# Seven copies out of PSUM moved from ScalarE to VectorE in the last four slots of an attention and soft-MoE kernel

## The chip, the cores and the metric

The kernel runs on one core of one Trainium2 chip. The metric is the device time of one execution, in microseconds (us). A core has TensorE (PE, matrix products into PSUM), VectorE (DVE), ScalarE (ACT), GpSimd (POOL) and SyncE (SP), each of which works through its own instructions in order; semaphores order them against each other. In this program POOL also issues every load, through one queue of DMA transfers (`gdma`).

## What is computed

Attention whose softmax has one more term in its denominator, then a soft mixture of experts with 8 experts of 4 slots each (32 slots):

```python
scores = scale * q @ k.T                       # 8 batches, 12 heads, 448 rows, 64 wide
m = max(scores, -1);  e = exp(scores - m)
x = (e / (sum(e, -1) + exp(-m) + 1e-9)) @ v    # then [3584, 768], heads side by side
logits = x @ phi                               # [3584, 32]
d = softmax of logits over all 3584 rows;  c = softmax of logits over the 32 slots
slot_input = d.T @ x
slot_out[expert] = relu(slot_input[expert] @ w1[expert]) @ w2[expert]
out = c @ slot_out
```

The softmax over all rows is made batch by batch with a running maximum; the weighted sum `d.T @ x` is corrected by a factor each time the maximum moves.

## The kernel before

**Pairs and slots.** The 96 heads are taken as 48 pairs n (`NPAIR`), six to a batch (`PB`), three to a group (`NP`, so `NG` is 16). The main loop (L556) has a slot s for every pair, and each slot has a first half (y=0) and a second half (y=1). For its pair a slot makes the scores with the maxima subtracted in PSUM (`Bk`: L300, then L303) and takes their exp on ACT (L306, four exps in the first half, three in the second). `AV` (L331) multiplies them with v into the one buffer of the pool psV. The maxima come from an earlier pass over the scores (`A`, with `reduce_max` on DVE at L229 and L238), which runs ahead of the slots and so has ended before the last four.

**What follows a pair.** `N1(n)` (L343) copies the pair's results out of psV; `N2(n)` divides them (the reciprocals L352 and L353 on DVE, the products L359, L367 and L368 on POOL, but on DVE for n from 44 on, see `on_pool` at L335). In slot s, N1(s-1) stands in the first half; N2(s-1) stands right behind it when it is on DVE, and at the end of the second half when it is on POOL. `PX(s-2)` in the second half turns the divided x over with four matmuls (L391) into a PSUM buffer of the pool psB, and L397 copies that to the tile `xT`. `W2` and `W3` turn a group's maxima into rows: L265 and L266 on PE, the copy at L271, two small exps at L274 and L277; group 16, the last, has its turn in slot 44.

**Buffers.** psB has four buffers handed out in turn. In the last slots the requests of one slot are: two for `Bk(s,0)`, two for `Bk(s,1)`, two for `Bk(s,2)`, one for `Bk(s,3)`, then one for `PX(s-2)` (in slot 44 `W2` takes one before it). So the buffer of `PX` is asked for again by the fourth request behind it, which is the second head's matmul of `Bk(s+1,1)`. psV has a single buffer: `AV` of the next pair waits for N1.

**Work hung between.** `post` (L511) holds the steps of the logits and of the running softmax of the batch that has just ended. For batch 6 they fall into slots 44 to 47: the logits and `c_max` (first half of 44), `l_turn` and `c_sub` (second half of 44), `s_max` and `d_sub` (first half of 45), the exps and `corr` (first half of 46), `s_mm` and `s_add` (second half of 46), `c_turn` (second half of 47, four short DVE instructions L475 to L479). In a half they are written ahead of PX. Batch 7, the last, follows in `last`: `l_mm` needs the columns of xT of pairs 42 to 47.

**Weights into freed space.** The weights of w2 for experts 3 to 7 are loaded into the tile R, which holds the attention's buffers until then. `part_at` (L554) and L629, L630, L644, L645 say which part goes when; each transfer waits until what lay there has been read. The parts are counted here in units of 192 KB (one index z of `load_part`). Those that matter below: five units after slots 44 and 45; five units after slot 46, into space that ends with x0, which `s_mm` of batch 6 reads (L469); two after slot 47; eight (L629, L630) after the last `AV` (they cover e2, e1 and vp1); four (L644) after the last read of xT; three (L645) after the last read of x1 by the last `s_mm`. The last matmuls of the experts (`slots(1)`, L669) read the end of that last part.

**The end.** `hidden`, `turn` and `slots` run the experts, and L728 to L739 make and store the output.

The pieces that the change touches are short:

```python
t = psm.tile([128, S], BF16, tag="mT", name="mT")
nc.scalar.copy(t, st["ps_m"][:, 0:S])                                    # W3, L271
(nc.scalar.copy if on_pool(n) else nc.vector.tensor_copy)(u, src)        # N1, L343
nc.scalar.copy(xT[:, pb, :], pss[0])                                     # PX, L397
```

Of the kernel before, what the change touches and what calls it, by code (L numbers as in the profile page):

```python
# [31 lines left out]
def kernel(  # L32
# [10 lines left out]
    nc = tc.nc  # L43
    B, H, S, D = q.shape
# [9 lines left out]
    NPAIR = B * PB  # L54
    NG = NPAIR // NP
# [40 lines left out]
    xT = part("xT", 0, KC * 512).rearrange("p (j s) -> p j s", j=KC)  # L96
# [25 lines left out]
    with ExitStack() as at:  # L122
# [62 lines left out]
        st = {"e2": 0}  # L185
# [82 lines left out]

        def W3(g):
            t = psm.tile([128, S], BF16, tag="mT", name="mT")  # L270
            nc.scalar.copy(t, st["ps_m"][:, 0:S])  # L271
            mT[g] = t
            e = psm.tile([128, NP, 7], F32, tag="ec", name="ec", bufs=3)
            nc.scalar.activation(e[:, :, 0:6].rearrange("p l (i h) -> p i l h", i=3),  # L274
                                 ngm[g][:, 0:18].rearrange("p (i l h) -> p i l h", i=3, h=2),
                                 AF.Exp, scale=scale)
            nc.scalar.activation(e[:, :, 6], ngm[g][:, 18:21], AF.Exp, scale=scale)  # L277
            ec[g] = e
# [56 lines left out]
        on_pool = lambda n: n < NPAIR - 4  # L335

        def N1(n):
            src = av[n][:, 0:7 * W65].rearrange("p (s c) -> p s c", c=W65)
            if n == NPAIR - 1:
                us[n] = src  # L340
                return
            u = ubuf[:, n % 2, :].rearrange("p (s c) -> p s c", c=W65)
            (nc.scalar.copy if on_pool(n) else nc.vector.tensor_copy)(u, src)  # L343
            us[n] = u

        def N2(n):
# [28 lines left out]
        def keep_busy(n):  # L375

            if "idle" not in st:
                st["idle"] = pb_("ps_idle")
            for _ in range(n):
                nc.tensor.matmul(st["idle"], ident, w_sb["w1", 0][:, 0, 0:512], start=True, stop=True)  # L380

        def PX(n):
            b, pb = divmod(n, PB)
            x, c = xb[b % 2], slice(pb * 128, pb * 128 + 128)
            two = n == NPAIR - 1
            pss = [pb_("ps_x") for _ in range(1 + two)]
            for i in range(4):
                if i == 3 and two:
                    keep_busy(1)
                o = (i % 2 if two else i) * 128  # L390
                nc.tensor.matmul(pss[i // 2 if two else 0][:, o:o + 128], x[:, i, c], ident if i < 3 else ident2,  # L391
                                 start=True, stop=True)
            if two:
                nc.scalar.copy(xT[:, pb, 0:256], pss[0][:, 0:256])
                nc.vector.tensor_copy(xT[:, pb, 256:512], pss[1][:, 0:256])
            else:
                nc.scalar.copy(xT[:, pb, :], pss[0])  # L397

# [142 lines left out]
        T(2)  # L543
        W2(0)
        W3(0)
        As(1)
        for nm in "qk":
# [8 lines left out]
        for s in range(NPAIR + 1):  # L556
            for y in range(2):
# [15 lines left out]
                if y == 0:  # L573
                    if 0 <= s - 1:
                        for i in (2, 3):
                            AV(s - 1, i, range(3))
                else:
                    if 2 <= s < NPAIR - 6:
                        T(s + 6)
                    g = (s + 1) // 3  # L580
                    if (s + 1) % 3 == 0 and g < NG:
                        W2(g + 1)
                        W3(g + 1)
                    if s < NPAIR:
                        for i in (0, 1):
                            AV(s, i, range(3))
                if 2 * s + y in post:
                    post[2 * s + y]()
                if y and 0 <= s - 2 < NPAIR - 2:
                    PX(s - 2)  # L590
                if y == 0:
                    if 0 <= s - 1:
                        for i in range(4):
                            AV(s - 1, i, [3])
                        N1(s - 1)
                        if not on_pool(s - 1):
                            N2(s - 1)
                else:
                    if 0 <= s - 1 and on_pool(s - 1):
                        N2(s - 1)  # L600
                As(early)
                if hs == 1:
                    W2(1)
                    W3(1)
                if hs == 4:
                    W1(2)
            g = (s + 10) // 3
            if s == 1 or s % 3 == 2:
                g = 3 if s == 1 else g
# [3 lines left out]
            g = (s + 9) // 3  # L613
# [16 lines left out]
        load_part(15, 0, 1)  # L630
        nc.vector.reduce_max(fold, ident.rearrange("p (i s) -> p s i", i=4), axis=AX.X)
        PX(NPAIR - 2)
        keep_busy(2)
        last[1]()
        PX(NPAIR - 1)
        keep_busy(1)
        last[2]()
# [50 lines left out]
        pss = [pb_("ps_so") for _ in range(2)]  # L688
# [26 lines left out]
    with ExitStack() as ex:  # L715
        psO = ex.enter_context(tc.tile_pool(name="psO", bufs=4, space=PSUM))
        for bp in range(B // 2):
# [4 lines left out]
            for t0 in range(0, 7, 2):  # L722
                ts = range(t0, min(t0 + 2, 7))
                pss = [psO.tile([128, 2, 512], F32, tag="o", name="ps_o") for _ in ts]
# [45 lines left out]
```

## Time and profile before

| what | value |
|---|---|
| time, median of 3 runs (lowest to highest) | 324.32 us (324.28 to 325.05) |
| the profiled execution | 326.12 us, span 324.3 us |
| busy: PE, DVE, ACT, POOL | 281.0, 257.5, 250.3, 199.3 us |
| in 250 to 270 us: PE, DVE, ACT, POOL | 18.0, 9.9, 17.8, 10.4 us |
| in the same 20 us: DMA | 143 GB/s, the mean of four windows of 5 us (122, 156, 173, 120) |
| in 270 to 285 us: DMA | 204 to 211 GB/s |
| slots 44, 45, 46, 47 begin (first L300) | 250.3, 255.7, 259.8, 265.05 us |
| output phase begins (first L728) | 294.31 us |

A span runs from the first to the last instruction of the profiled execution; the execution's own time has 1.8 us around it. Start times of the trace are given in us from the span's start. In a row of the time line the first number is the start, the second the duration of the merged group, and in brackets stands the idle time before it with what ended it. A chain of waits is read from its end: each piece was released by the one above it.

### The profile page before, as it was taken

Reading aid. Unit: us, or ns where it says so; the run is one execution under the profiler, and the core shown is the slowest. Engines: PE = TensorE matmul, PEld = TensorE weight load, DVE = VectorE, ACT = ScalarE, POOL = GpSimd, SP = SyncE. Lnnn points to the kernel's source line nnn. Section 1 sums busy time; section 2 is a strip of 40 time slices with the busy share of each in tenths; the row PEclk is TensorE's granted clock in tenths of the full one; section 3 lists DMA queues with packets and bytes.
Section 4 is the critical chain, followed back from the end, with each engine's and each line's share of the span. In section 5 each row is a group of like instructions: output and inputs, shape, how many; then the busy total and the mean of one; then the engine's idle time right before and its main releaser. Section 6 shows DMA issues by size and latency. Waiting matters only on the chain.

```text
span 324.3 us, 12137 instructions
## 1 busy us (share of the span) xinstructions
PE 281.0 (87%) x5052; PEld 162.5 (50%) x5054; DVE 257.5 (79%) x601; ACT 250.3 (77%) x547; POOL 199.3 (61%) x399
## 2 busy tenths in 40 slices
PE   3898899999999999999999999999899887977800
PEld 1444456556656565556656565656565444441100
DVE  4779999998999899899999998999899355327910
ACT  2456699998999899989998999899989984317800
POOL 8641778888787869666978688777747825000000
PEclk9999999999999999999999999999999999998555
DMA  6990599999999999866999999999646889973997
GB/s 86 140 133 3 86 205 152 202 166 193 173 174 176 176 187 150 135 98 113 149 196 132 196 158 193 148 200 146 111 51 99 140 137 194 210 131 160 434 424 340
DMA packets 42438, 54.30 MB, mean 167 GB/s; under 512 B 2576, under 2 KB 35344, under 8 KB 42000
## 3 DMA queue, kind: packets, MB, share of 16 engines
q0 software_dynamic: 41376, 42.52, 84.7%
q1 hardware_dynamic: 1008, 11.01, 8.1%
q8 instruction: 39, 0.64, 0.7%
q14 instruction: 15, 0.12, 0.1%
HBM read 85.03 MB, written 11.01 MB: 296 GB/s over the span
## 4 chain that ended last, share of the span: by engine, by line
PE 35%; DVE 29%; ACT 18%; issue 6%; DMA 4%; POOL 3%; POOLq 0%; ACTq 0%
DVE mx L229 18%; ACT R L306 9%; PE ps_av L331 8%; PE ps_a L225 6%; PE ps_b L300 6%; PE ps_t L203 5%; DMA R<-in_moe_w_dram 4%; PE ps_b L303 4%; ACT R L206 3%; DVE mx L238 3%; ACT R L397 2%; PE ps_o L728 2%; DVE R L208 2%; ACT W L734 2%; PE ps_s L469 2%
## 5 line engine op out<-in xcount | busy, mean ns | idle before, releaser
L229 DVE TENSOR_REDUCE mx<-ps_a 128x1 f32<-128x448 f32 x288 | 160.9, 614 | 13.2 <-PE ps_a L225 12.7
L306 ACT ACTIVATE R<-ps_b 128x448 bf16<-128x448 f32 x336 | 158.6, 563 | 12.9 <-PE ps_b L303 8.6
L300 PE MATMUL ps_b<-R 64*128 64x448 bf16 (+1 forms) x384 | 83.2, 360 | 3.2 <-ACT R L397 3.0
L303 PE MATMUL ps_b<-mT,sel 64*128 64x448 bf16 (+1 forms) x384 | 79.0, 354 | 0.0
L225 PE MATMUL ps_a<-R 64*128 64x448 bf16 x288 | 68.6, 369 | 5.8 <-DVE mx L229 3.4
L331 PE MATMUL ps_av<-R 128*128 128x65 bf16 (+1 forms) x1536 | 64.9, 196 | 2.0 <-DVE ubuf L343 1.3
L359 POOL TENSOR_TENSOR R<-ubuf,rec 128x384 bf16<-128x384 f32 x44 | 36.1, 821 | 49.2 <-DVE rec L353 39.6
L331 PEld LDWEIGHTS <-R 128*128 128x128 bf16 (+1 forms) x1536 | 50.7, 101 | 27.5 <-issue 23.4
L203 PEld LDWEIGHTS <-R 64*64 64x64 bf16 x1344 | 31.4, 113 | 19.6 <-issue 9.6
L203 PE MATMUL ps_t<-ident,R 64*64 64x64 bf16 x1344 | 31.9, 198 | 7.7 <-DMA R<-in_q_dram 4.0
L397 ACT CAST R<-ps_x 128x512 bf16<-128x512 f32 x47 | 28.3, 601 | 10.3 <-PE ps_x L391 10.3
L303 PEld LDWEIGHTS <-sel 64*128 64x128 bf16 (+1 forms) x384 | 21.5, 98 | 24.5 <-issue 17.8
L300 PEld LDWEIGHTS <-R 64*128 64x128 bf16 (+1 forms) x384 | 19.7, 97 | 27.4 <-issue 22.9
L238 DVE TENSOR_REDUCE mx<-ps_a 128x1 f32<-128x448 f32 x48 | 29.5, 614 | 0.6 <-PE ps_a L235 0.3
L206 ACT COPY R<-ps_t 128x896 bf16<-128x896 bf16 x20 | 18.4, 919 | 11.0 <-PE ps_t L203 11.0
L343 ACT COPY ubuf<-ps_av 128x455 f32<-128x455 f32 x44 | 25.2, 572 | 2.1 <-PE ps_av L331 1.0
L225 PEld LDWEIGHTS <-R 64*128 64x128 bf16 x288 | 17.8, 94 | 15.0 <-issue 4.1
L368 POOL TENSOR_TENSOR R<-ubuf,rec 128x128 bf16<-128x128 f32 x44 | 17.5, 398 | 3.7
L235 PE MATMUL ps_a<-R 64*64 64x448 bf16 x96 | 18.7, 386 | 0.6 <-DVE mx L229 0.6
L391 PE MATMUL ps_x<-ident,R 128*128 128x128 bf16 x192 | 18.7, 219 | 0.0
L245 POOL TENSOR_SCALAR R<-mx 64x6 bf16<-64x6 f32 (+5 forms) x51 | 13.5, 264 | 8.4 <-DVE mx L229 4.8
L108 POOL DMA_DIRECT2D R<-in_moe_w_dram x15 | 10.7, 717 | 12.3 <-PE ps_s L469 7.2
(121 smaller groups left out, 364.8 us busy)
## 6 DMA issues: line engine op xcount, KB each, us to landing
W<-in_moe_w_dram POOLq DMA_DIRECT2D x22, 768.0 KB, 9.4
out_dram<-W SPq DMA_DIRECT2D x3, 2688.0 KB, 11.2
R<-in_v_dram POOLq DMA_DIRECT2D x32, 192.0 KB, 4.5
R<-in_q_dram POOLq DMA_DIRECT2D x15, 336.0 KB, 6.9
R<-in_k_dram POOLq DMA_DIRECT2D x15, 336.0 KB, 7.8
R<-in_moe_w_dram POOLq DMA_DIRECT2D x3, 768.0 KB, 9.4
out_dram<-W SPq DMA_DIRECT2D x3, 768.0 KB, 4.3
R<-in_moe_w_dram POOLq DMA_DIRECT2D x1, 1344.0 KB, 13.3
```

Of the source, the lines that this page charges most:

```text
L203: nc.tensor.transpose(ps[r, a, c:c + 64], src[r, pl, tok * D:(tok + 1) * D], ident[r, r])
L206: nc.scalar.copy(t, ps)
L225: nc.tensor.matmul(pss[hl][:, 0:S], t[r, 0, i * 128:(i + 1) * 128], t[r, 1, :], start=True, stop=True)
L229: nc.vector.reduce_max(mx[g][:, c:c + 1], pss[hl][:, 0:S], axis=AX.X)
L238: nc.vector.reduce_max(mx[g][:, c:c + 1], ps[:, 0:S], axis=AX.X)
L300: nc.tensor.matmul(outs[hl], t[rs[hl], 1, cols], t[rs[hl], 0, :], start=True, stop=False)
L303: nc.tensor.matmul(outs[hl], sel[rs[hl], 2 * pl + hl:2 * pl + hl + 1].to_broadcast([64, m]), mT[mg(n)][rs[hl], :], start=False, stop=True)
L306: nc.scalar.activation(e, p[:, 0:S], AF.Exp, scale=scale)
L331: nc.tensor.matmul(o, eT[n, i, hl][:, qc], vp[g % 2][:, 2 * pl + hl, i, 0:W65], start=(i == 0 and u == 0 and hl == 0), stop=(i == 3), skip ...
L343: (nc.scalar.copy if on_pool(n) else nc.vector.tensor_copy)(u, src)
L359: eng.tensor_mul(x[:, 0:3, c:c + 128].rearrange("p i (h d) -> p i h d", h=2), u[:, 0:6, 0:D].rearrange("p (i h) d -> p i h d", h=2), rec[: ...
L397: nc.scalar.copy(xT[:, pb, :], pss[0])
```

## The change

Three copies get a condition of their own. The copy of a group's maxima's rows goes to DVE for the last group (g = 16: one instruction). The copy of a pair's results goes to DVE from n = 43 on, where it was from n = 44 on (one more instruction; pairs 44 to 46 were there already, and pair 47 has no copy). The copy of transposed x goes to DVE for n = 42 to 46 (five instructions); pair 47 keeps its two half copies, one on each engine. Where the products of N2 run is not changed.

```diff
         def W3(g):
             t = psm.tile([128, S], BF16, tag="mT", name="mT")
-            nc.scalar.copy(t, st["ps_m"][:, 0:S])
+            (nc.scalar.copy if g < NG else nc.vector.tensor_copy)(t, st["ps_m"][:, 0:S])
...
-            (nc.scalar.copy if on_pool(n) else nc.vector.tensor_copy)(u, src)
+            (nc.scalar.copy if n < NPAIR - 5 else nc.vector.tensor_copy)(u, src)
...
-                nc.scalar.copy(xT[:, pb, :], pss[0])
+                (nc.scalar.copy if n < NPAIR - 6 else nc.vector.tensor_copy)(xT[:, pb, :], pss[0])
```

## The prediction

> **What bounds the kernel now.** I read the busy shares of the page first, then the stretch that the change touches (250 to 272 us) in windows, then the chain of waits there, then the time lines of DVE, ACT and PE, and last the DMA rate. The windows (PE, PEld, DVE, ACT, POOL, granted clock, DMA share, GB/s):
>
> ```profile
> 250.00:255.00 5.00, 4.42 (x78) 2.42 (x75) 1.08 (x4) 4.97 (x12) 4.33 (x12) 1.00 0.77 122
> 255.00:260.00 5.00, 4.60 (x75) 2.56 (x73) 3.07 (x11) 4.64 (x13) 3.88 (x8) 1.00 0.96 156
> 260.00:265.00 5.00, 4.09 (x80) 2.42 (x76) 2.70 (x10) 3.95 (x10) 0.23 (x1) 1.00 1.05 173
> 265.00:270.00 5.00, 4.88 (x92) 2.94 (x89) 3.07 (x12) 4.24 (x9) 1.98 (x3) 1.00 0.79 120
> ```
>
> ACT looks full and DVE half idle, so a move seems free. But the chain says who waits for whom:
>
> ```profile
> 256.24 0.19 PE ps_b L300
> 256.43 0.35 PE ps_b L300
> ...
> 259.64 0.24 PE ps_x L391 x4
> ...
> 259.90 0.58 ACT R L397
> 260.48 1.76 ACT R L306 x4
> ...
> 262.99 0.64 DVE ubuf L343
> ...
> 263.67 0.52 PE ps_av L331 x12
> 264.19 0.69 PE ps_s L469 x28
> ...
> 277.54 13.89 DMA R<-in_moe_w_dram
> ```
>
> Two things are to be seen. First, a slot here is a latency chain through PE, ACT and DVE, about 4.1 to 5.4 us long. The exps of a slot begin at most 0.1 us after their matmuls: in slot 45 L303 ends at 256.24 and the exp starts at 256.27, in slot 46 260.34 and 260.38, in slot 47 265.60 and 265.63. So ACT has hardly a queue in front of them that the change could empty. In slot 44 W2 waits for POOL (its last maxima row ends at 254.77, L266 starts at 254.82), which no moved copy feeds. Second, the second head's L300 of Bk(s+1,1) waits for the buffer that PX used: it starts at 256.43, 260.53 and 265.79, 0.05 us behind the ends of the L397 copies (256.38, 260.48, 265.73). PE is in order, so everything behind it waits too. In groups the page has the same:
>
> ```profile
> L300 PE MATMUL ps_b<-R 64*128 64x448 bf16 (+1 forms) x384 | 83.2, 360 | 3.2 <-ACT R L397 3.0
> ```
>
> The end is then set by the load of the last weights, 13.89 us in the chain. Those DMAs run without a gap at about 207 GB/s, or 0.95 us a unit, from 267.5 to 288.4 us (22 units), so their end follows their first gate, s_mm in slot 46 (issue at 265.06, data from about 267.5: 2.45 us later). PE, which works through the experts meanwhile, is close behind:
>
> ```profile
> 288.75 1.97 PE L669 MATMUL ps_so<-R,W 128*32 128x384 bf16 x43
> 291.47 1.14 PE L669 MATMUL ps_so<-R,W 128*32 128x384 bf16 x21 [0.76 <-DMA R<-in_moe_w_dram]
> ```
>
> The last matmul before the gap starts at 290.39, and the next of its group of four at 291.47, so PE has 1.08 us to spare there.
>
> **The change, part by part.** Seven copies leave ACT: N1(43) 0.54, mT 0.53, five xT of 0.59 to 0.61, some 4.0 us. By the first observation this gains at most 0.1 us a slot, and I take nothing. A gain bounded by ACT's queue is the second rival.
>
> On DVE the price of a cast of 512 columns out of PSUM is not in the trace. The nearest rows are 256 columns 0.425 us (L395) and 384 columns 0.557 us (L676); the line through them gives 0.69 for 512 and 0.63 for the 448 of mT. N1 is in the trace (455 columns, 0.62). As bounds for the xT copy I keep 0.58 (as on ACT) and 0.80. The Trainium skill, VectorE: DVE Perf Modes, section on the TRN2 errata, gives 120 cycles plus one a column for PSUM into SBUF at 0.96 GHz, an estimate of 0.66 us; by it the 384 columns would take 0.53, where the trace has 0.557, and the sum below would come out about 0.13 lower (the step from 0.58 to 0.80 below moves it by 0.95).
>
> What counts is not the price but the **place in DVE's order**. An xT copy stands in the second half of its slot, behind everything that DVE has for the first half, and from slot 45 on this is N1 and the whole of N2:
>
> ```profile
> 258.44 0.62 DVE L343 COPY ubuf<-ps_av 128x455 f32<-128x455 f32 x1
> 259.10 0.17 DVE L352 SCALAR_TENSOR_TENSOR rec<-ubuf,ec 128x7 f32<-128x7 f32 x1
> 259.30 0.20 DVE L353 RECIPROCAL rec<-rec 128x7 f32<-128x7 f32 x1
> 259.53 0.56 DVE L359 TENSOR_TENSOR R<-ubuf,rec 128x384 bf16<-128x384 f32 x1
> 260.01 0.22 DVE L367 TENSOR_SCALAR rec<-halfm,rec 128x2 f32<-128x2 f32 x1
> 260.26 0.29 DVE L368 TENSOR_TENSOR R<-ubuf,rec 128x128 bf16<-128x128 f32 x1
> ```
>
> It ends at 260.56, when the copy on ACT has been over for 0.08 us. Replayed by rows (an independent DVE instruction starts 0.08 before the one ahead ends):
>
> - Slot 44. N1(43) waits for nobody of weight: AV(44) is behind W2. mT 255.08 to 255.71, in time for L303 at 255.89. Behind it on DVE: sm (needs ps_lT, 255.53) starts at 255.63 for 255.57, c_sub ends at 256.12, xT(42) runs 256.04 to 256.74, where ACT ended at 256.38: +0.36. The reciprocals of N2(43), queued behind it, are some 0.7 late, and so is POOL behind them with x(43) and five DMA units at 258.19; x(43), at 258.8, is still there ahead of PX(43) at 259.8.
> - Slot 45. PE is 0.36 late from Bk(45,1) on, so s_max, N1(44) and N2(44) are too: L368 ends at 260.92, xT(43) runs 260.84 to 261.54 against 260.48: +1.06.
> - Slot 46. L303 of the first head of Bk(46,1) ends at 261.96, its exp starts at 262.01 instead of 261.24: +0.78, for ACT had 0.3 in hand. Corr, N1(45), AV(46), s_mm and the first DMA gate follow: **+0.78** (265.84). xT(44) queues behind N2(45) and s_add: 266.11 to 266.81 against 265.73: +1.08.
> - Slot 47. N1(46), which waits for PE, and N2(46) are +1.08, c_turn (L475 to L479) stands ahead of xT(45) as well: L479 ends at 271.03 for 269.95, xT(45) runs 270.95 to 271.65 against 269.51: +2.14. In l_mm column 3 needs it: 271.70 for 269.58, and AV(47)'s last part stands behind: +2.12.
> - After the loop. N2(47) and the fold (L631) +2.12; xT(46) at 273.56 to 274.26, where ACT ended at 272.33 (there it waited for the two L365, so DVE makes good 0.2): **+1.93** for the whole chain to the experts.
>
> At the end: PE is late by 1.93 - 1.08 = 0.85. The DMAs: first gate +0.78; seven units from 268.3 last to 274.95; the eight units behind AV(47), issued at 270.63, go at 272.75 and have data from 275.2, a hole of 0.25; so +0.78 to +1.05. The four and the three units are issued at 276.3 and 279.5, long before their turn. The larger of the two sets slots(1): +0.85 to +1.05, I take **+0.95**. The output phase only moves: its DMAs run at about 410 GB/s from 297 us on. With 0.58 and 0.80 for the copy the same replay gives +0.5 and +1.45.
>
> The sum is made against the span of 324.3 us (profiled time 326.12, so 1.8 around it). The median of the runs shown is 324.32; a shift of 0.95 on the same program carries over: 325.3 us.
>
> **Rivals.**
>
> *A hole in the loads.* If the DMA queue runs dry before the eight units are issued, the end follows their gate instead of the first: +2.12, 326.4 us. For it: the two gates are only 0.25 us from this. Against: 0.95 us a unit has held for 22 units. It decides once AV(47) is more than 0.3 us later than replayed, or the units go faster.
>
> *Faster: ACT's queue.* If the exps of slot 44 and 45 were held by ACT's fullness (4.97 of 5 us in 250 to 255), the 1.4 us of N1(43), mT and xT(42) would come out of slot 44 and bring s_mm's gate and all the DMAs forward by that: 322.9 us. It decides if POOL's maxima rows came before 254.0 and DVE were free to take xT at once. Against: POOL's 254.77 and the 0.03 us between matmul and exp. The Trainium skill, TensorEngine Tiling (Array Packing), PSUM Bottleneck, advises to use both engines to empty PSUM; that speaks for this case, and the idle DVE in the windows (9.9 of 20 us) agrees with it, but the order above decides.
>
> *Hidden.* The late copies eat the slack of the exps and of the loads: within 0.3 us of now, 324.3 to 324.6. For it: 0.3 in hand on ACT, 1.08 on PE. Against: s_mm's gate has none, and even without slot 44's 0.36 N2(44)'s end at 260.56 puts xT(43) 0.7 late, and the gate 0.4.
>
> **Chances.** Forecast (+0.5 to +1.45) 0.70; hole 0.10; hidden 0.12; faster 0.08. A difference of 0.3% (0.97 us, so 325.29) is about what a measurement of this kernel can tell from no change, and the forecast lies on it. Of the forecast's 0.70 I put 0.42 above, since small waits between queued copies are not in the replay, and 0.28 below. Slower: 0.42 + 0.10 = 0.52. Within: 0.28 + 0.12 = 0.40. Faster: 0.08. The range leaves the faster case out and takes in hidden and hole: 324.2 to 326.5.
>
> **What would show it.** Right: on DVE L397 at about 0.69 us, starting behind L368 in slots 45 to 47; the second L300 of a slot idle for DVE's L397, by some 0.4, 1.1 and 1.1 us; s_mm about 0.8 later; l_mm waiting for xT; the gap before the last L669 matmuls gone or near it, or the last load landing at about 292.4. Wrong: if the exps of slot 44 or 45 start over 0.3 us earlier than now, if xT(43) starts before N2(44) has ended, or if the loads end where they do now.

## The result, and the profile after

The changed kernel took 326.98 us (median of 6 runs, 326.46 to 327.55) against 324.3 us (6 runs, 323.29 to 325.05) in the same measurement: ratio 1.0084, 95% interval 1.0060 to 1.0107. A second measurement on another occasion gave 1.0059 (1.0035 to 1.0083). So it is slower by 0.6 to 0.8%, about 2 to 2.7 us, where 0.95 us was forecast; the time lies above the forecast range.

The span of its profiled execution is 325.3 us, and the forecast for the median time was 325.3 us too. That agreement is luck: a span is 1.8 us shorter than the time (this execution took 327.12 us), and the profile of before (time 326.12, span 324.3 us, slot 44 beginning about 1 us later) belonged to one of its slower executions; a second profile of the same kernel has a span of 322.9 us. From here on profiles are therefore laid over each other at the **first exp of slot 44**, up to which the programs are the same: 251.01 us in the first profile of before, 249.86 in the second, 250.04 in that of the changed kernel.

The chain of waits of the changed kernel (start, duration, what; L398 is L397 of before, L301 is L300, L418 is L417) now runs through the moved copies. A piece counts in it only from the end of the one before it, so the copies, which take 0.68 us, stand here with about 0.6:

```profile
255.11 0.61 DVE R L398
255.76 0.35 PE ps_b L301
...
264.88 0.61 DVE R L398
265.54 0.35 PE ps_b L301
...
269.70 0.59 DVE R L398
270.33 0.27 PE ps_l L418 x4
...
272.29 0.61 DVE R L398
272.95 0.29 PE ps_l L418 x4
...
276.63 2.13 PE ps_idle L381 x5
278.76 0.71 PE ps_s L470 x28
```

The upper two pairs are the waits that the prediction named: a score matmul that waits for the buffer of a late xT copy. The next two are the columns of l_mm that wait for xT(45) and xT(46). The last two lines are the surprise: five filler matmuls (`keep_busy`, whose results nobody uses) take 2.13 us, where they took 1.24 from 274.98 on in the first profile of before. The windows of the changed kernel (PE, PEld, DVE, ACT, POOL, granted clock, DMA share, GB/s) say why:

```profile
270.00:272.00 2.00, 1.28 (x18) 0.71 (x18) 1.31 (x6) 0.00 (x0) 0.60 (x1) 1.00 1.16 210
272.00:274.00 2.00, 1.05 (x10) 0.78 (x11) 0.89 (x3) 0.89 (x3) 1.86 (x6) 0.51 0.99 177
274.00:276.00 2.00, 1.96 (x10) 0.70 (x8) 0.71 (x2) 0.27 (x1) 0.76 (x2) 0.50 0.88 135
276.00:278.00 2.00, 2.00 (x7) 0.82 (x6) 0.81 (x4) 0.35 (x2) 0.17 (x1) 0.50 1.12 192
```

TensorE's granted clock is 0.50 from 272.0 us for 6.8 us; in the first profile of before it was 1.00 throughout this stretch. Such a stretch is called a dip below. The last column shows a second thing: the loads, at 210 GB/s up to 272 us, sink to 135 for a while. The queue ran dry, as one of the rivals had it; whether the end followed is answered further down.

All times below are us after the first exp of slot 44; "column 4" and "column 5" are the matmuls of l_mm that need xT(45) and xT(46) (columns 3 and 4 where the prediction and the expectation of g count from 0), "experts" the first matmul of slots(1), "output" the first of the output phase.

| kernel | s_mm, batch 6 | column 4 | column 5 | last s_mm | experts | output | clock at 0.5 |
|---|---|---|---|---|---|---|---|
| before, first profile | 13.01 | 18.57 | 21.38 | 25.50 | 37.73 | 43.30 | none |
| before, second profile (a) | 13.04 | 18.59 | 21.40 | 26.33 | 38.56 | 43.06 | 3.4 us |
| changed, first | 13.47 | 20.30 | 22.91 | 28.52 | 40.81 | 45.32 | 6.8 us |
| changed, second (n) | 13.50 | 20.34 | 22.95 | 28.12 | 40.38 | 44.88 | 3.4 us |
| xT copies alone (b) | 13.51 | 20.34 | 22.95 | 28.07 | 40.36 | 45.61 | 3.4 us |
| all but xT (c) | 12.97 | 18.53 | 21.34 | 26.23 | 38.46 | 42.97 | 3.4 us |
| changed, fillers in both waits (d) | 13.47 | 20.30 | 22.92 | 27.05 | 39.28 | 43.78 | none |
| xT 42 to 44 alone (f) | 13.51 | 19.34 | 22.15 | 26.28 | 38.51 | 43.01 | none |
| xT 45 and 46 alone (g) | 13.01 | 19.56 | 22.17 | 27.02 | 39.25 | 43.76 | 3.4 us |
| changed, PX earlier (h) | 13.50 | 18.76 | 21.36 | 25.49 | 37.71 | 42.36 | none |
| f with other buffers (m) | 12.88 | 18.20 | 21.01 | 25.14 | 37.37 | 41.93 | none |

The output phase takes 30.0 us from its first matmul in every one of them.

### The profile page after: what moved, and what is told of

The parts are those of the page before. It is cut to its first block, busy times and chain, and to the rows that moved or that the text cites. A ratio compares the mean times of both kernels' runs of the same rounds, so it can differ in the third digit from the quotient of the medians.

```text
span 325.3 us, 12138 instructions
## 1 busy us (share of the span) xinstructions
PE 282.8 (87%) x5054; PEld 163.4 (50%) x5054; DVE 261.9 (80%) x608; ACT 247.1 (76%) x540; POOL 199.7 (61%) x399
## 4 chain that ended last, share of the span: by engine, by line
PE 41%; DVE 30%; ACT 16%; issue 5%; POOL 3%; POOLq 0%; ACTq 0%
DVE mx L229 16%; ACT R L307 8%; PE ps_av L332 8%; PE ps_a L225 6%; PE ps_b L301 6%; PE ps_t L203 5%; PE ps_b L304 4%; ACT R L206 3%; DVE mx L238 3%; ACT W L735 2%; ACT R L398 2%; PE ps_o L729 2%; DVE R L208 2%; PE ps_h L656 2%; PE ps_so L670 2%
## 5 line engine op out<-in xcount | busy, mean ns | idle before, releaser
L301 PE MATMUL ps_b<-R 64*128 64x448 bf16 (+1 forms) x384 | 83.2, 360 | 4.0 <-ACT R L398 2.7
L301 PEld LDWEIGHTS <-R 64*128 64x128 bf16 (+1 forms) x384 | 19.7, 97 | 27.1 <-issue 22.7
L398 ACT CAST R<-ps_x 128x512 bf16<-128x512 f32 x42 | 25.3, 603 | 8.7 <-PE ps_x L392 8.7
```

The lines of the kernel that those rows point to most:

```text
L301: nc.tensor.matmul(outs[hl], t[rs[hl], 1, cols], t[rs[hl], 0, :], start=True, stop=False)
L398: (nc.scalar.copy if n < NPAIR - 6 else nc.vector.tensor_copy)(xT[:, pb, :], pss[0])
```

## The experiments

The theory after the result: the five xT copies, late by their place on VectorE, make TensorE wait (1.5 us up to column 5); the waits in l_mm set off a dip of the granted clock, which stretches what follows (in these profiles by 0.8 to 1.5 us). Each ratio is to the kernel before, run beside it.

**(a) The kernel before again.** No edit.

> The kernel before, unchanged, for the scatter of its time and a second profile. All theories: ratio 1.000, interval within 0.5% on both sides. If the first profile (span 324.3 us, slot 44 beginning at 250.3 us) was an unusually late one, this one has a span of 322.2 to 323.5 us; granted clock 1.0 until the output phase, as there. If the span is again 324.3 us while the times stay at 324.3 us, the profile is simply 1.8 us slower than a timed run.

Ratio 1.0003 (0.9982 to 1.0025), span 322.9 us: the first profile was a late one. It also brought what was not expected: the kernel before has a dip of its own, of 3.4 us, in this execution and not in the other. So does c.

**(b), (c) The change in two parts.** In b only the xT line of the change, in c the other two.

```diff
 b:
-                nc.scalar.copy(xT[:, pb, :], pss[0])
+                (nc.scalar.copy if n < NPAIR - 6 else nc.vector.tensor_copy)(xT[:, pb, :], pss[0])
 c:
-            nc.scalar.copy(t, st["ps_m"][:, 0:S])
+            (nc.scalar.copy if g < NG else nc.vector.tensor_copy)(t, st["ps_m"][:, 0:S])
-            (nc.scalar.copy if on_pool(n) else nc.vector.tensor_copy)(u, src)
+            (nc.scalar.copy if n < NPAIR - 5 else nc.vector.tensor_copy)(u, src)
```

> Only the five copies of transposed x go to VectorE; the copy of pair 43's results and of the last maxima's rows stay on ScalarE. Theory (the xT copies queue behind N2 on VectorE, l_mm waits for them, TensorE idles and its granted clock falls to 0.5 around 272 us for some 7 us): all of the loss is here, ratio 1.006 to 1.010, with the stretch at clock 0.5 ahead of 280 us in the profile. Rival (the other two copies carry a share, through the maxima's rows on the way to slot 45 or the results of pair 43 on the way to AV): ratio at most 1.005.

> Only the copy of pair 43's results and that of the last maxima's rows go to VectorE; the xT copies stay on ScalarE. Theory: ratio 0.998 to 1.001, granted clock 1.0 until the output phase. Rival (these two carry a share): ratio 1.002 or more. If ScalarE's queue in slot 44 did matter, the ratio is under 0.997.

b: 1.0077 (1.0049 to 1.0105); c: 1.0000 (0.9981 to 1.0019). The loss is in the xT copies, as far as these intervals tell; that ScalarE was relieved of the other two gained nothing.

**(d), (e), (o) The clock.** Fillers where TensorE waits in l_mm: d has them in both waits of the changed kernel, e in the same places of the kernel before, o in the changed kernel ahead of column 5 alone.

```diff
-            return [lambda: l_mm(range(PB - 2)),
+            return [both(lambda: l_mm(range(PB - 3)), lambda: keep_busy(4), lambda: l_mm([PB - 3])),   # d, e
...
         PX(NPAIR - 2)
-        keep_busy(2)
+        keep_busy(8)                                                                                # d, e, o
```

> The changed kernel with ten more of its filler matmuls (results unused) where TensorE waits for xT in the last batch: four ahead of the fourth column of l_mm, six more ahead of the fifth. Theory with the clock gate: no stretch at clock 0.5 ahead of the output phase, the filler matmuls at 0.21 us each instead of 0.43, the last s_mm some 1 us earlier than in the changed kernel, ratio to before 1.002 to 1.006. Rival (the clock has no part, order on VectorE is all): ratio stays at 1.008 or is higher by the filler's own time.

> The kernel before with the same ten filler matmuls (results unused) in the two waits of l_mm. Theory (the loss is made of two terms, the order on VectorE and the dip of TensorE's granted clock that the waits in l_mm set off): no dip to 0.5 ahead of the output phase, the chain from slot 44 to the experts some 0.8 us shorter than in the second profile of before, which had a dip of 3.4 us; ratio 0.996 to 1.000, and so the changed kernel with fillers (1.0051) is 0.5 to 0.9% above its like: that is the order's share. Rival (the clock costs nothing, fillers are what changed): ratio 1.000 or over, with the same chain as before.

> The changed kernel with fillers only in the second of the two waits of l_mm, ahead of the fifth column (six more), none in the first, which the change has lengthened to about 1 us. If the second wait, which the kernel before has as well, sets off the dip, it is gone: no stretch at 0.5 in the profile, ratio 1.003 to 1.006 as with fillers in both. If the first wait does, the dip stays in most runs: ratio 1.006 to 1.009, mean granted clock at or under 0.955.

d: 1.0051 (1.0025 to 1.0076). No dip; the time line of its PE has the fillers at full pace:

```profile
268.45 1.02 PE L381 MATMUL ps_idle<-W,ident 128*128 128x512 bf16 x4
...
270.13 1.89 PE L381 MATMUL ps_idle<-W,ident 128*128 128x512 bf16 x8
...
274.65 1.24 PE L381 MATMUL ps_idle<-W,ident 128*128 128x512 bf16 x5
```

Up to column 5 d is the changed kernel to 0.01 us (table), and from there it is 1.5 us faster to the experts than the first profile of the changed kernel, and 1.1 than the second. In these profiles that is the dip's price. o: 1.0047 (1.0024 to 1.0070), no dip in the profile, and in all its runs a mean granted clock of at least 0.956, where the second measurement of the changed kernel had at most 0.955 in all 12 (the first had 0.956 and 0.960 in two of its 6). In the profiles here an execution without a dip has 0.957 or more, one with a dip at most 0.954. So fillers in the second wait suffice, as the first of its two expectations had it. e: 0.9998 (0.9973 to 1.0023). No dip in the profile, but its chain is no shorter than that of a, because here xT(45) is in time and the four fillers only push column 4 back, by 0.83 us (19.42). From column 5 to the experts it takes 16.35 us, as without a dip elsewhere, so the two cancel. As a control for the clock alone e therefore failed; that it equals before says little.

What d and o keep, 0.5%, is the order's share, with the later loads in it. How much of the median the dip takes is shown less well. The intervals of d and o overlap those of the changed kernel; all 21 runs of d and o together lie 0.8 us in the median under the 24 of the changed kernel and b. But four of these 24 have no dip by their mean granted clock (0.956 to 0.961), and they take 326.55 to 327.78 us, no less than the others.

**(f), (g), (m) Which xT copies, and by which way.** f moves the copies of pairs 42 to 44, which are held against slots 45 to 47; g those of 45 and 46, which l_mm needs at once; m is f with the buffers of these PX from another pool.

```diff
 f, g:
-                nc.scalar.copy(xT[:, pb, :], pss[0])
+                (nc.vector.tensor_copy if n in (42, 43, 44) else nc.scalar.copy)(xT[:, pb, :], pss[0])   # g: (45, 46)
 m, besides f:
-            pss = [pb_("ps_x") for _ in range(1 + two)]
+            pss = [psA.tile([128, 512], F32, tag="a", name="ps_x")] if n in (42, 43, 44) else [pb_("ps_x") for _ in range(1 + two)]
```

> Of the five xT copies only those of pairs 42, 43 and 44 go to VectorE. If the loss is made by the PSUM buffers that late xT copies hold in slots 45 to 47 (the step of the prediction), this kernel has most of it: s_mm of batch 6 later by 0.5, the l_mm stage by 0.7 to 1.1 us against slot 44, ratio 1.003 to 1.006. If it is made at the end, where l_mm waits for xT(45) and xT(46), this kernel has little: ratio 1.000 to 1.002.

> Only the xT copies of pairs 45 and 46 go to VectorE. Buffers in slots 45 to 47 as before, so s_mm of batch 6 unmoved; but xT(45) queues behind N2(46) and c_turn, and column 3 of l_mm waits about 1.0 us, column 4 about 0.8. If the loss is made at the end, with the clock: ratio 1.003 to 1.007, a dip of 3.4 or 6.8 us in the profile. If it is made by the buffers: 1.000 to 1.002.

> The kernel in which the xT copies of pairs 42 to 44 alone are on VectorE, with the PSUM buffers of these three taken from the other pool (psA, idle there since the maxima are done) and not from psB. If a late copy costs through the psB buffer that it holds, the second head's score matmul waits no longer: s_mm of batch 6 back from 13.5 to 12.9 to 13.2 us after the first exp of slot 44, l_mm from 19.0 to 18.3 to 18.6, ratio 0.998 to 1.001. If it costs in another way (VectorE's own queue ahead of N1), s_mm stays at 13.5.

f: 1.0015 (0.9990 to 1.0040), g: 1.0030 (1.0009 to 1.0050). Neither of the two pure answers: column 5 is late by 0.76 in f and by 0.78 in g, and 0.76 + 0.78 = 1.54 is what the changed kernel has (22.92 - 21.39 = 1.53). The buffers and the copies that l_mm needs share the order's loss in halves; in time f is not clear of before, and g, whose profile has the dip, is. By their mean granted clock six of f's 12 runs have a dip too: their median is 325.54 us, that of the other six 324.26.

The time line of f's PE shows the second head's matmul of slots 45, 46 and 47 waiting:

```profile
256.53 0.35 PE L300 MATMUL ps_b<-R 64*128 64x448 bf16 x1 [0.29 <-DVE R L397]
...
261.16 0.35 PE L300 MATMUL ps_b<-R 64*128 64x448 bf16 x1 [0.44 <-ACT R L306]
...
266.38 0.35 PE L300 MATMUL ps_b<-R 64*128 64x448 bf16 x1 [0.28 <-DVE R L397]
```

In m the same stretch has both heads together, and the wait is gone:

```profile
254.72 0.35 PE L300 MATMUL ps_b<-R 64*128 64x448 bf16 x2
...
258.68 0.35 PE L300 MATMUL ps_b<-R 64*128 64x448 bf16 x2
...
263.93 0.35 PE L300 MATMUL ps_b<-R 64*128 64x448 bf16 x2
```

m: 0.9978 (0.9950 to 1.0005), s_mm back at 12.88, column 5 at 21.01, earlier than in before. So the buffer is the way by which these three copies cost. Since m takes three requests off psB, part of its gain can be that; the kernel before with the same buffers was not run.

The middle line of f corrects the account of the kernel given above: the buffers of psB are not always handed out in turn. The second head of slot 46 starts there at 261.16 us, when an exp has ended, and before the copy of xT(43) ends at 261.56; so it has another buffer than that of PX, one that an exp has read. In the changed kernel it is the same (start at 260.33, end of xT(43) at 260.72). Why the buffer is another one there is not shown.

**(h) The same copies in another place.** All seven on VectorE, but PX of pairs 44 and 45 written in the first half of slots 46 and 47, ahead of `post` and N1.

```diff
+                early_px = NPAIR - 2 <= s < NPAIR
+                if y == 0 and early_px:
+                    PX(s - 2)
                 if 2 * s + y in post:
                     post[2 * s + y]()
-                if y and 0 <= s - 2 < NPAIR - 2:
+                if y and 0 <= s - 2 < NPAIR - 2 and not early_px:
                     PX(s - 2)
```

> The changed kernel, but PX of pairs 44 and 45 is written in the first half of slots 46 and 47, ahead of post and N1, so that the two xT copies stand in front of N1 and N2 on VectorE (N1 of 45 and 46 come up to 0.6 us later for it). Theory (the place in VectorE's order makes the loss, not VectorE's 0.69 us as such): l_mm no longer waits for xT(45); ratio 1.000 to 1.004. Rival (the copies cost through VectorE's longer time alone): ratio stays at 1.006 to 1.010.

Ratio 0.9988 (0.9965 to 1.0012), a little under the range expected: the loss is gone with the engine unchanged. The gain is in l_mm (column 5 at 21.36, as in before); s_mm stays at 13.50, since PX of pairs 42 and 43 stands where it stood. With the wait ahead of column 4 gone its profile has no dip (two of its 12 runs have one by their mean granted clock), so h takes away the order's loss at the end and the dip together. VectorE's time line has xT(45) ahead of N1(46):

```profile
266.97 0.69 DVE L398 CAST R<-ps_x 128x512 bf16<-128x512 f32 x1 [1.06 <-PE ps_x L392]
267.57 0.62 DVE L344 COPY ubuf<-ps_av 128x455 f32<-128x455 f32 x1
```

In the changed kernel the same copy stood behind N2(46) and c_turn:

```profile
268.67 0.29 DVE L369 TENSOR_TENSOR R<-ubuf,rec 128x128 bf16<-128x128 f32 x1
...
269.52 0.18 DVE L480 RECIPROCAL crec<-crec 128x4 f32<-128x4 f32 x1
269.62 0.66 DVE L398 CAST R<-ps_x 128x512 bf16<-128x512 f32 x1
```

**(n) The changed kernel again.**

> The changed kernel again, for a second profile and a closer ratio. Theory (order on VectorE, then the clock's dip): ratio 1.006 to 1.010; against the first exp of slot 44 the order's part repeats to 0.1 us (s_mm of batch 6 at 13.5, the fourth column of l_mm at 20.3, the fifth at 22.9), while the dip of the granted clock differs from execution to execution, 3.4 or 6.8 us long, and moves the experts' start with it. Rival (the dip of 6.8 us belongs to the kernel): the same dip at the same place.

Ratio 1.0059 (1.0035 to 1.0083), at the lower end of the range expected. The order's part repeats to 0.04 us, the dip does not: 3.4 us long and 2.8 us later than in the first profile. The rival, a dip fixed to the kernel, is out.

**(j), (k), (p), (q) Versions to beat both.** The same idea, turned on the kernel before: N1 of pairs 44 and 45 queues behind steps of batch 6 on VectorE, which can stand behind it.

```diff
 j (on before), k (on h), q (on m); all three with keep_busy(8) as in o. p is m with keep_busy(8) alone.
+                behind = y == 0 and s in (NPAIR - 3, NPAIR - 2)
-                if 2 * s + y in post:
+                if 2 * s + y in post and not behind:
                     post[2 * s + y]()
...
                         if not on_pool(s - 1):
                             N2(s - 1)
+                        if behind:
+                            post[2 * s]()
```

> A version to beat both: the kernel before (copies on ScalarE) with the batch-6 steps of the first halves of slots 45 and 46 written behind N1 and N2, so that N1(44) and N1(45) no longer queue behind them on VectorE, and six more filler matmuls in the wait ahead of the fifth column of l_mm, where TensorE idles anyway. Theory: s_mm of batch 6 and its DMA gate 0.8 to 1.2 us earlier against slot 44, the chain to the experts as much earlier, no dip or a short one; ratio 0.993 to 0.998. Rival (the loads end where they end): s_mm earlier, end unmoved, ratio 0.999 or over.

> The same two edits on the changed kernel with PX of pairs 44 and 45 ahead of N1 (all seven copies on VectorE). Theory: like the one above if VectorE's order is right in all slots, ratio 0.993 to 0.999; but xT(43) still stands behind N2(44) and now also behind s_max and d_sub, so slot 46 may lose 0.3 to 0.6 us against it.

> The kernel with the xT copies of pairs 42 to 44 on VectorE and their PSUM buffers from the other pool, with the same six fillers ahead of the fifth column. Without them 9 of its 12 runs had a mean granted clock of at most 0.954 and a median of 324.83 us, and the three others 322.65 us. If the dip is what separates these, the fillers leave the second sort alone: median 322.4 to 323.2 us, ratio 0.993 to 0.997. If the scatter has another source, the ratio stays at 0.998 to 1.000.

> The one above with the batch-6 steps of the first halves of slots 45 and 46 behind N1 and N2. If the order on VectorE sets the chain, the 1.1 us that this edit gave on the kernel before comes on top in part: s_mm of batch 6 at 11.7 to 12.2 us after the first exp of slot 44, ratio 0.990 to 0.995. If the loads set the end by then, the ratio stays at 0.994 to 0.997 and the experts' last matmuls wait for the load.

j: 0.9957 (0.9933 to 0.9981), 323.35 us; k: 0.9963 (0.9935 to 0.9991); q: 0.9964 (0.9945 to 0.9984); p: 0.9994 (0.9966 to 1.0022). j beats both kernels with the copies left on ScalarE: s_mm at 11.91. It has fillers besides the new order; e, with more of them in the old order, gained nothing. k's s_mm comes at 12.85, so its slot 46 loses 0.94 us against j, more than the 0.3 to 0.6 expected. q has the shortest chain of all (s_mm 11.17, experts 35.66) and gains nothing by it over j: its last matmuls wait for the load, as its second expectation had it.

```profile
289.55 1.14 PE L672 MATMUL ps_so<-R,W 128*32 128x384 bf16 x21 [1.35 <-DMA R<-in_moe_w_dram]
```

p missed: 11 of its 12 runs have no dip by their mean granted clock (0.956 to 0.960), and they still scatter from 322.87 to 326.09 us, so the two sorts of runs of m are not made by the dip alone. What else does it is left open; the end of the loads, which differs between executions with the same gates (next section), is a candidate that was not tried by itself.

## Why the prediction was wrong

Direction and place were right; what ends the chain, and so the size, was not.

- **ACT relieved gains nothing.** Right: the first exp of slot 45 comes 5.26 us after that of slot 44 in both kernels, though three copies have left ScalarE by then, and c equals before.
- **The price of the copy.** Right: 0.683 us (median of five) for 0.69, mT 0.625 for 0.63.
- **Slots 45 to 47.** Right in kind. xT(42) ends 0.30 later (0.36 said), xT(43) 1.21 (1.06 said), but s_mm only 0.46 (0.78 said): in slot 46 the second head did not wait for xT(43), whose buffer it was said to need. xT(44) follows with 0.73 (1.08 said).
- **l_mm.** Column 4 came 1.73 late for 2.12, column 5 1.53 for 1.93: still 0.4 less than said, as xT(44). m and f show the buffers' half of it, g the other, h the order as its cause.
- **"PE is late by 1.93 - 1.08 = 0.85."** This is the step that failed, on both sides of the minus sign. (1) The 1.08 us in hand were read from one execution, in which the load landed late. There the last packet of the weights is at 40.14; in the second profile of before and in c, with the first gates at 14.07 and 14.00 for 14.05, it is at 38.94 and 38.68. PE, with the first profile's chain, needs that load at 39.4 (37.73 and 1.64 of matmuls). In the first profile it went on 0.32 after the last packet, so with these two loads it could go on at 39.3 and 39.0, and would not have waited: nothing was in hand. In a and in the changed kernel PE, not the load, ends the chain: both have the 64 matmuls without a wait, where the first profile had 43 and 21 (a, then changed):

```profile
288.42 2.78 PE L669 MATMUL ps_so<-R,W 128*32 128x384 bf16 x64
...
290.85 2.78 PE L670 MATMUL ps_so<-R,W 128*32 128x384 bf16 x64
```

  h shows the same from another side: with the experts at 37.71, as in the first profile of before, and the last packet at 39.21, its output starts 0.94 sooner (42.36 for 43.30).

  (2) The chain behind l_mm was taken to move as it stood, which put a change of the clock at nothing. It was stretched by the dip: from column 5 to the experts it takes 16.35 us without a dip (first profile of before; d 16.36), 17.2 in a, 17.4 in n and 17.9 in the changed kernel's first profile.
- **The hole in the loads**, which the forecast put at 0.25 us and the rival at more: it came. The eight units are issued 1.74 later (21.36 for 19.62), with the first gate only 0.45 later, and the rate sinks to 135 GB/s. But the end did not follow by 2.12, as that rival had it. The last packet is at 40.21 and 40.86 in the two profiles of the changed kernel, 39.79 in d, 41.81 in o, 42.45 in b; the first profile of before had 40.14. That the loads end where they did was one of the prediction's own signs of being wrong. In o and b the last matmuls wait for it (0.89 and 0.44 us), in the changed kernel PE ends last. Which of the two is later varies by execution; their shares in the median are not settled.
- **The sum by what was measured.** With fillers against the dip the changed kernel is slower by 1.4 us (d 325.99 against 324.60, o 325.83 against 324.43); without them it takes 326.7 to 327.0, another 0.7 to 1.2, of which the dip's part is open, as said at d and o. The kernel before pays for its own dips less: of 124 of its runs, 60 have a mean granted clock of at most 0.955 and a median of 324.60, the other 64 have 324.36.

The range was too narrow for the same two reasons: the price of the copy, which was known well, made both ends of the forecast's shift, and nothing allowed for how one execution differs from the next.

## What to carry to other kernels

When work moves to an idle engine, ask where in that engine's order it comes to stand and who waits for it, not how full the engine is: the seven copies cost 0.6 to 0.8% with every late xT copy behind N2, and nothing that could be measured once two of them stood ahead of it. A slack read at the end of one profile is a property of that execution; take a second profile of the same kernel before subtracting it. And look at what a new wait does to TensorE's granted clock in the work behind it.

## What the runs showed of the hardware that was not expected

The granted clock fell to 0.50 in the middle of the work, for 3.4 or 6.8 us, though TensorE never stood idle for long: around the start of the dip it was 0.85 and 1.34 us at a time in the changed kernel and 1.55 us in a and c (the lines are of the changed kernel, the last one of a):

```profile
269.03 0.46 PE L418 MATMUL ps_l<-phi_sb,R 128*128 128x32 bf16 x12
270.33 0.27 PE L418 MATMUL ps_l<-phi_sb,R 128*128 128x32 bf16 x4 [0.85 <-DVE R L398]
...
272.95 0.29 PE L418 MATMUL ps_l<-phi_sb,R 128*128 128x32 bf16 x4 [1.34 <-DVE R L398]
...
271.26 0.29 PE L417 MATMUL ps_l<-phi_sb,R 128*128 128x32 bf16 x4 [1.55 <-ACT R L397]
```

The times at which the clock changes lie whole multiples of 3.41 us apart within an execution, and the start of the grid differs between executions. In the 3.41 us ahead of each of the six dips seen (changed kernel twice, a, b, c, g) PE was busy for 0.48 to 0.60 of the time. But stretches of 0.53 (first profile of before), 0.55 (m) and 0.61 (h) passed without one, so no bound can be read from these. Nor is it that both gaps must fall into one such stretch: in n and b the gap of 0.85 lies ahead of it, and in the kernel before there is one gap of 1.55 us, with a dip in a and without one in the first profile. Why the kernel before has a dip in some executions only is open.

The Trainium skill, TensorE: Matmul & The Clock Gate, Part 1, describes windows of about 3.4 us after which the clock is halved or released; the lengths of 3.4 and 6.8 us agree. The Trainium skill, TensorE: Matmul & The Clock Gate, section Why this matters for your kernels, asks that no idle gap between matmuls exceed some 3 us if the clock is not to fall; here it fell after single gaps of 1.33 us (n), 1.34 us (b) and 1.55 us (a, c), and the measurement decides.
